# A hand-written order for the second slot of a fused attention and Gelu-MLP kernel

## The chip, the cores and the metric

The kernel runs on one core of one Trainium2 chip. A core has five engines with an instruction queue each: TensorE (PE) for matmuls, VectorE (DVE), ScalarE (ACT), GpSimd (POOL) and SyncE (SP), which here only issues transfers. They run side by side and wait for each other through semaphores. The metric is the device time of one execution in microseconds (us).

## The reference

For each of 8 batches and 8 heads, 512 tokens `x` and 32 state vectors attend to each other; then all 8 × (512 + 32) = 4352 rows, each with the 8 heads side by side (512 numbers), go through a two-layer network with an exact Gelu.

```python
scores = scale * np.matmul(x, state.transpose(0, 1, 3, 2))
a = softmax(scores);   xread = np.matmul(a, state)        # 512 rows a batch
scores2 = scale * np.matmul(state, x.transpose(0, 1, 3, 2))
a2 = softmax(scores2); sread = np.matmul(a2, x)           # 32 rows a batch
x = concatenate([xread, sread], axis=2)  # heads side by side: 4352 x 512
h = x @ w_in                             # w_in 512 x 2048
g = 0.5 * h * (1.0 + erf(h * inv_sqrt2))
return g @ w_out                         # w_out 2048 x 512
```

## The kernel before, in words

All matmuls take bf16 inputs. Instead of forming `xread` and multiplying it by `w_in`, the kernel multiplies the state by `w_in` first: `P = state @ w_in` for each batch (`p_mm`, in four chunks of 512 columns), and then `h = a @ P`. One step of `mm1(b, m)` makes 128 of the 2048 hidden columns for the 512 tokens of a batch: two matmuls (line 478) and one Gelu on ACT (line 485) into `g`. `M(k, ...)` in the code calls `mm1` for the global column block k = 16 × batch + m. The second product of batches 0 and 1 is done in units of four matmuls (`mm2`, line 504): `U(u)` is one unit, for a quarter q of the hidden columns and a quarter j of the rows, where u = 16 × batch + 4 × q + j. The last quarter of a row block is copied out of PSUM by DVE (line 491) and written by SP. From batch 2 on the second product is done by `X`, a scheme with seven block products instead of eight; it needs sums of quarters of `w_out` (`w_sums`, five DVE additions at line 552) and of `g` (`g_sum`, line 580).

The attention of a batch b is prepared one slot ahead. `rearr` (POOL, line 218) puts the tokens into the order that a transposing transfer wants, `xtr_dma` (SP, line 271) transposes them into `xT`, and `rearr_ones` (POOL, line 228) makes the copy `xo` that the state read uses. `scores` makes 16 small matmuls in two halves (line 324) and an exponential on ACT for each half (line 331). `norm` sums, inverts and multiplies on DVE (lines 344, 346 and 347), and `atr_dma` (SP, line 367) transposes the result `a` into `AT`, which `mm1` of that batch reads. `pmat(b, f)` makes one chunk of P: eight matmuls (line 415) and two casts out of PSUM, one on ACT (line 426) and one on DVE (line 427).

The exponential and the Gelu use different function tables of ACT: a table load (1.28 us in the profile) stands ahead of the first of each kind.

Every engine works in the order in which the calls are written; the file fixes this order by hand and there is no planner. A "slot" is the time in which a batch's sixteen M are done, in eight steps of two. The kernel uses eight PSUM tiles of 128 × 512 float32. Four of them (`ps_f`) rotate among the outputs of M, the scores, P chunks and small transposes: the n-th output takes the place of the (n-4)-th and waits until that has been read. The other four (`otile`) hold the second product's sums; some P chunks borrow them as well.

The change concerns the second slot (batch 1's M, numbers 16 to 31), from step 2 on. It is a loop over p = 2 to 7 after line 920. In it `hold` and `load_x(4)` (POOL, the latter a transfer of a batch of tokens) are issued once; the small copy `hold` keeps POOL back until a Gelu has been done, so that the load starts no sooner. After that loop the general one over b = 2 to 7 begins. In its first pass the remaining units of batch 1 are done, two in each of the steps 0 to 3 and one in each step from 4 on, until there are none left. The P chunks of batch 3 come in steps 5 and 7 (`p_run`), the first two of them in borrowed ones.

Of the kernel before, what the change touches and what calls it, by code (L numbers as in the profile page):

```python
# [17 lines left out]
def kernel(  # L18
# [8 lines left out]
    nc = tc.nc  # L27
# [51 lines left out]
    hold = persist.tile([128, 1], BF16, name="hold")  # L79
# [35 lines left out]
    def load_x(b):  # L115
        xb = xin.tile([128, H, SJ * D], BF16, name="xb", tag="xb")
        nc.gpsimd.dma_start(out=xb, in_=xr[b])
        xbs[b] = xb
# [80 lines left out]
    def begin(b):  # L199
        A = Att()  # L200
        atts[b] = A
        A.x4 = x4s[b % 2]
        A.xo = xos[b % 2]
        if b > 0:
            A.xT = att.tile([128, SJ, HC, 128], BF16, name="xT", tag="xT")

    def begin_e(b):
        A = atts[b]
        A.e = att.tile([128, SJ * 2, HC * NS], BF16, name="e", tag="e")
        A.a = att.tile([128, SJ * 2, HC * NS], BF16, name="a", tag="a")  # L210
# [3 lines left out]
    def rearr(b):  # L214
        A = atts[b]
        src = xbs[b].rearrange("p (t c) (j d) -> p t c j d", t=2, d=D)
        for t in range(2):
            nc.gpsimd.tensor_copy(  # L218
                out=A.x4[:, :, :, 64 * t:64 * t + 64].rearrange("p j c d -> p c j d"),
                in_=src[:, t],  # L220
            )

    def rearr_ones(b):
        A = atts[b]
        eng = nc.vector if b < 2 else nc.gpsimd
        src = xbs[b].rearrange("p (t c) (j d) -> p t c j d", t=2, d=D)
        for t in range(2):
            eng.tensor_copy(  # L228
                out=A.xo[:, :, :, 2 + 64 * t:66 + 64 * t].rearrange("p j c d -> p c j d"),
                in_=src[:, t],  # L230
            )
# [37 lines left out]
    def xtr_dma(b):  # L269
        A = atts[b]  # L270
        nc.sync.dma_start_transpose(
            out=A.xT.rearrange("p j c n -> p (j c) n"),
            in_=A.x4.rearrange("p j c n -> p (j c n)"),
        )
# [41 lines left out]
    def scores(b, half):  # L316
        A = atts[b]
        if half == 0:
            begin_e(b)
        pt = ps_f.tile([128, SJ, 2, 2, NS], FP32, name="pt", tag="f")  # L320
        for ci in range(2):
            c = 2 * half + ci
            for j in range(SJ):
                nc.tensor.matmul(  # L324
                    pt[:, j, :, ci, :],
                    lhsT=A.xT[:, j, c, :],
                    rhs=sbd[:, b, c, :],
                    start=True,
                    stop=True,
                )  # L330
        nc.scalar.activation(  # L331
            out=A.e[:, :, 64 * half:64 * half + 64],
            in_=pt.rearrange("p j t c n -> p (j t) (c n)"),
            func=AF.Exp,
            scale=scale,
        )

    def norm(b, half):
        A = atts[b]
        G = SJ * 2  # L340
        hs = slice(64 * half, 64 * half + 64)
        e4 = A.e[:, :, hs].rearrange("p g (c n) -> p g c n", n=NS)
        cs = att.tile([128, G, 2], FP32, name="cs", tag="cs")
        nc.vector.reduce_sum(out=cs, in_=e4, axis=AX.X)  # L344
        ics = att.tile([128, G, 2], FP32, name="ics", tag="ics")
        nc.vector.reciprocal(out=ics, in_=cs)
        nc.vector.tensor_tensor(  # L347
            out=A.a[:, :, hs].rearrange("p g (c n) -> p g c n", n=NS),
            in0=e4,
            in1=ics[:, :, :].to_broadcast((128, G, 2, NS)),  # L350
            op=ALU.mult,
        )
# [11 lines left out]
    def atr_dma(b):  # L364
        A = atts[b]
        A.AT = att.tile([128, SJ, 2, 128], BF16, name="AT", tag="AT")
        nc.sync.dma_start_transpose(
            out=A.AT.rearrange("p j t n -> p (j t) n"), in_=A.a
        )
# [29 lines left out]
    def srt(b):  # L399
        A = atts[b]  # L400
        ps = ps_f.tile([128, HC, NS], BF16, name="srT", tag="f")
        nc.tensor.transpose(
            ps.rearrange("p c n -> p (c n)"), A.srm.rearrange("q t d -> q (t d)"), ident
        )
        nc.vector.tensor_copy(out=XSR[:, :, :, b], in_=ps)  # L405
# [18 lines left out]
    def p_copy(b, f, ps):  # L424
        dst = Ps[b][:, :, f * 512:(f + 1) * 512]
        nc.scalar.copy(out=dst[:, 0, :], in_=ps[0])  # L426
        nc.vector.tensor_copy(out=dst[:, 1, :], in_=ps[1])  # L427

    def pmat(b, f):
        p_copy(b, f, p_mm(b, f, ftile))  # L430
# [40 lines left out]
    gs = {}  # L471
# [82 lines left out]
    def w_sums(i):  # L554
        (b11, b12), (b21, b22) = w_q
        w_add(*(
            ("3", b12, b22, ALU.subtract),
            ("4", b21, b11, ALU.subtract),
            ("6", b11, b12, ALU.add),
            ("1", b11, b22, ALU.add),  # L560
            ("7", b21, b22, ALU.add),
        )[i])
# [245 lines left out]
    def M(*ms):  # L808
        for m in ms:
            mm1(m // MC, m % MC)  # L810

    def U(*us):
        for u in us:
            mm2(u // 16, u % 16 // 4, u % 4)
# [105 lines left out]
    U(16)  # L920


    u = 17
    for p in range(2, 8):
        if p == 4:
            scores(2, 0)
            scores(2, 1)
            norm(2, 0)
            norm(2, 1)
        if p == 7:  # L930
            atr_dma(2)
        if p == 3:
            begin(3)
            rearr(3)
            xtr_dma(3)
            rearr_ones(3)
        M(16 + 2 * p, 17 + 2 * p)
        U(u)
        u += 1
        if p in (5, 7):  # L940
            pmat(2, 2 + p // 7)
        if p >= 3:
            w_sums(p - 3)
        if p == 2:
            nc.gpsimd.tensor_copy(out=hold, in_=gs[1][:, 4, 0:1])
            load_x(4)

    for b in range(2, B):
        nb = b + 1
        for p in range(8):  # L950
            k = 16 * b + 2 * p
            if p == 1 and nb < B:
                scores(nb, 0)
                scores(nb, 1)
            if p in (2, 3) and nb < B:
                norm(nb, p - 2)
            if p == 3 and nb + 1 < B:
                xtr_dma(nb + 1)
            if p == 5 and nb < B:
                atr_dma(nb)  # L960
            if p == 3 and nb < B:
                srt(b)
            if p == 7 and nb == B - 1:
                srt(nb)
            M(k, k + 1)
            if b == 2:
                for _ in range(2 if p < 4 else 1):
                    if u < 32:
                        U(u)
                        u += 1  # L970
            elif p < 5:
                if p == 0:
                    g_sum(b - 1, "5")
                X(b - 1, "45127"[p])
                if p < 3:
                    g_sum(b - 1, "127"[p])
            if nb == B and p < 4:
                for m in range(4 * p, 4 * p + 4):
                    mm1_sr(m)
            if p == 1 and nb < B:  # L980
                sread(b)
                sread_out(b)
            if p == 4 and nb == B - 1:
                sread(nb)
                sread_out(nb)
            if p == 0 and b + 3 < B:
                nc.gpsimd.tensor_copy(out=hold, in_=gs[b][:, 0, 0:1])  # L987
                load_x(b + 3)
            if p == 0 and nb + 1 < B:
                begin(nb + 1)  # L990
                rearr(nb + 1)
            if p == 2 and nb + 1 < B:
                rearr_ones(nb + 1)
            if nb == B:
                if p == 4:
                    r_homes()
                    r_sum("5")
                    r_sum("2")
                if p == 5:
                    g_sum(b, "6")  # L1000
                    R("3")
                    r_sum("1")
                    R("4")
                    r_sum("6")
                    r_sum("7")
                if p == 6:
                    R("5")
                    X(b, "3")
                    R("2")
                    R("1")  # L1010
                if p == 7:
                    R("6")
                    X(b, "6")
                continue
            if p == 5:
                g_sum(b, "6")
                if nb < B:
                    p_run(nb, (0, 1), ((0, 1), (3, 2)))
            if p == 6:
                X(b, "3")  # L1020
            if p == 7:
                if nb < B:
                    p_run(nb, (2, 3), ((1, 2), None))
                X(b, "6")
# [41 lines left out]
```

The softmax here doesn't subtract the row's maximum and nothing guards it: scores larger than these inputs give would overflow.

## Time and profile before

| quantity | value |
|---|---|
| time, median of 13 runs | 209.8 us (209.3 to 211.76) |
| time of the profiled execution | 209.8 us |
| its span, first to last instruction | 208.0 us |
| busy: PE, DVE, ACT, POOL | 96%, 66%, 64%, 30% |
| granted PE clock, mean | 0.997 |
| start of M(20, 21), start of M(32, 33) | 42.02 us, 55.21 us |

A line of the timeline gives the start and the length in us, the engine, the line of the kernel, the operation, what it writes and reads, the shapes, and how many instructions are merged in it; in brackets stands the idle time of the engine before it and what ended that. Matmuls overlap, so the step from one start to the next is what a matmul costs. A line of a tile's view gives the shortest, median and longest duration in ns, then the first and last start.

### The profile page before, as it was taken

To read this page: it belongs to the slowest core of one execution; us is meant where nothing else is said; L and a number is where in the kernel's file an instruction comes from. 1 tells how busy PE (TensorE), PEld (TensorE's weight loads), DVE (VectorE), ACT (ScalarE), POOL (GpSimd) and SP (SyncE) were. 2 spreads that over 40 slices of the span, in tenths; PEclk is the share of its full clock that TensorE was granted. 3 is DMA by queue.
4 is the path that set the end of the run, shared out by engine and by line. 5 is a ranking of instruction groups with operands and counts; after the bars stand their busy time and mean duration, and the time that the engine had idled before them with its cause. 6 is when DMAs were issued, how large, how long until landed. Compare 5 with 4: busy or idle time off the path is not lost.

```text
span 208.0 us, 4691 instructions
## 1 busy us (share of the span) xinstructions
PE 200.6 (96%) x1963; PEld 131.2 (63%) x1971; DVE 137.4 (66%) x218; ACT 133.2 (64%) x240; POOL 62.1 (30%) x69
## 2 busy tenths in 40 slices
PE   7899999998999999999999999999999999999993
PEld 6545444453454567756775677757775788778882
DVE  2944675747919648995699658855887553165872
ACT  3864875679794779565956777587757566744120
POOL 8964300664171015710677005600220001200000
PEclk9999999999999999999999999999999999999998
DMA  6999999689373908736582603360106001030124
GB/s 191 199 181 204 205 195 192 108 221 192 50 99 96 262 0 102 155 123 82 60 167 59 174 0 87 69 202 3 52 3 202 3 0 50 3 151 0 54 102 151
DMA packets 40261, 23.14 MB, mean 111 GB/s; under 512 B 21808, under 2 KB 38320, under 8 KB 40240
## 3 DMA queue, kind: packets, MB, share of 16 engines
q0 software_dynamic: 13936, 8.10, 28.7%
q1 hardware_dynamic: 25616, 14.36, 26.6%
q10 hardware_dynamic: 688, 0.39, 0.6%
q8 instruction: 15, 0.25, 0.5%
q14 instruction: 6, 0.05, 0.1%
HBM read 17.30 MB, written 8.91 MB: 126 GB/s over the span
## 4 chain that ended last, share of the span: by engine, by line
PE 74%; DVE 11%; DMA 5%; POOL 4%; ACT 3%; issue 1%; POOLq 0%; DVEq 0%; ACTq 0%
PE xp L586 28%; PE hp L478 21%; PE op L504 9%; DMA w_out_bf<-in_moe_w_out_dram 5%; DVE gsum L580 5%; PE p_ps L415 4%; PE hps L518 3%; PE rp L764 3%; DVE a L347 2%; POOL w_in_bf L105 2%; PE op L531 2%; DVE cs L344 1%; PE sr L378 1%; POOL sbd L95 1%; PE pt L324 1%
## 5 line engine op out<-in xcount | busy, mean ns | idle before, releaser
L485 ACT ACTIVATE g<-hp 128x512 bf16<-128x512 f32 x124 | 67.6, 602 | 31.6 <-PE hp L478 26.5
L478 PE MATMUL hp<-AT,P 128*128 128x512 bf16 x248 | 64.2, 379 | 0.5 <-DVE XSR L405 0.4
L586 PEld LDWEIGHTS <-gsum 128*128 128x128 bf16 x464 | 45.0, 98 | 11.5 <-issue 2.1
L580 DVE TENSOR_TENSOR gsum<-g 128x2048 bf16<-128x2048 bf16 x30 | 39.3, 1328 | 0.1
L478 PEld LDWEIGHTS <-P 128*128 128x128 bf16 x248 | 22.3, 98 | 21.2 <-issue 4.0
L586 PE MATMUL xp<-ws,gsum 128*128 128x256 bf16 x272 | 32.5, 273 | 0.0
L427 DVE CAST P<-p_ps 128x512 bf16<-128x512 f32 x31 | 20.0, 684 | 15.8 <-PE p_ps L415 15.8
L504 PE MATMUL op<-w_out_bf,g 128*128 128x512 bf16 x90 | 23.0, 379 | 0.4 <-DMA w_out_bf<-in_moe_w_out_dram 0.2
L586 PE MATMUL xp<-ws,g 128*128 128x256 bf16 x192 | 22.9, 273 | 0.0
L586 PE MATMUL xp<-w_out_bf,gsum 128*128 128x256 bf16 x192 | 22.8, 273 | 0.0
L586 PEld LDWEIGHTS <-g 128*128 128x128 bf16 x192 | 18.8, 98 | 4.3
L426 ACT CAST P<-p_ps 128x512 bf16<-128x512 f32 x31 | 16.9, 602 | 6.9 <-PE p_ps L415 6.9
L635 POOL TENSOR_TENSOR u<-s,oh 128x512 f32<-128x512 f32 x5 | 6.3, 1267 | 49.0 <-ACT oh L632 49.0
L504 PEld LDWEIGHTS <-g 128*128 128x128 bf16 x96 | 9.1, 98 | 11.7 <-issue 1.4
L218 POOL COPY x<-xb 128x1024 bf16<-128x1024 bf16 x12 | 12.6, 1083 | 11.3 <-DMA xb<-in_x_dram 11.3
L228 POOL COPY xo<-xb 128x1024 bf16<-128x1024 bf16 x12 | 14.5, 1241 | 1.3 <-PE sr L378 1.3
L347 DVE TENSOR_TENSOR a<-e,ics 128x512 bf16<-128x512 bf16 x14 | 13.9, 994 | 0.5
L344 DVE TENSOR_REDUCE cs<-e 128x16 f32<-128x512 bf16 x14 | 9.5, 677 | 3.8 <-ACT e L331 3.8
L415 PE MATMUL p_ps<-w_in_bf,sbd 64*32 64x512 bf16 x248 | 11.1, 382 | 0.8 <-ACT g L485 0.7
L605 POOL TENSOR_TENSOR v<-q,oh 128x512 f32<-128x512 f32 x5 | 6.4, 1277 | 14.8 <-ACT oh L637 14.8
L629 DVE TENSOR_TENSOR s<-xp,s 128x512 f32<-128x512 f32 x5 | 3.5, 692 | 11.0 <-PE xp L586 11.0
L987 POOL COPY hold<-g 128x1 bf16<-128x1 bf16 x3 | 1.0, 332 | 31.5 <-ACT g L485 31.5
(111 smaller groups left out, 221.2 us busy)
## 6 DMA issues: line engine op xcount, KB each, us to landing
xb<-in_x_dram POOLq DMA_DIRECT2D x7, 512.0 KB, 6.7
out_dram<-oh SPq DMA_DIRECT2D x13, 256.0 KB, 2.5
out_dram<-osb SPq DMA_DIRECT2D x10, 256.0 KB, 3.3
out_dram<-oh SPq DMA_DIRECT2D x5, 512.0 KB, 2.7
w_out_bf<-in_moe_w_out_dram POOLq DMA_DIRECT2D x4, 512.0 KB, 12.2
w_in_bf<-in_moe_w_in_dram POOLq DMA_DIRECT2D x6, 256.0 KB, 11.9
x0f<-in_x_dram SPq DMA_DIRECT2D x3, 256.0 KB, 4.0
w_in_bf<-in_moe_w_in_dram POOLq DMA_DIRECT2D x4, 128.0 KB, 3.9
```

Of the source, the lines that this page charges most:

```text
L218: nc.gpsimd.tensor_copy(out=A.x4[:, :, :, 64 * t:64 * t + 64].rearrange("p j c d -> p c j d"), in_=src[:, t],)
L228: eng.tensor_copy(out=A.xo[:, :, :, 2 + 64 * t:66 + 64 * t].rearrange("p j c d -> p c j d"), in_=src[:, t],)
L344: nc.vector.reduce_sum(out=cs, in_=e4, axis=AX.X)
L347: nc.vector.tensor_tensor(out=A.a[:, :, hs].rearrange("p g (c n) -> p g c n", n=NS), in0=e4, in1=ics[:, :, :].to_broadcast((128, G, 2, NS) ...
L415: nc.tensor.matmul(ps[t][32 * c:32 * c + 32, :], lhsT=sbd[64 * t:64 * t + 64, b, c, 32 * t:32 * t + 32], rhs=w_in_bf[64 * t:64 * t + 64, c ...
L426: nc.scalar.copy(out=dst[:, 0, :], in_=ps[0])
L427: nc.vector.tensor_copy(out=dst[:, 1, :], in_=ps[1])
L478: nc.tensor.matmul(hp, lhsT=Ps[b][:, t, m * 128:(m + 1) * 128], rhs=atts[b].AT[:, :, t, :], start=(t == 0), stop=(t == 1),)
L485: nc.scalar.activation(out=gs[b][:, m, :], in_=hp, func=AF.Gelu)
L504: nc.tensor.matmul(ps, lhsT=gs[b][:, m, j * 128:(j + 1) * 128], rhs=w_out_bf[:, m, :], start=(m == 0), stop=(m == MC - 1),)
L580: nc.vector.tensor_tensor(out=t, in0=g_q(b, h0, k0), in1=g_q(b, h1, k1), op=op)
L586: nc.tensor.matmul(ps[:, j - js[0], :], lhsT=lhs[:, m, 128 * j:128 * j + 128], rhs=rhs[:, m, :], start=(first and j == js[0] and m == 0), ...
```

## The change

The loop over steps 2 to 7 of the second slot is written out, in another order. The chunk `pmat(2, 2)` moves from step 5 to ahead of M(22, 23). The scores of batch 2 come behind M(22, 23) directly, ahead of U(18). U(20) and U(21) stand together behind M(26, 27), and U(23), which was in the next slot, is done ahead of M(32, 33). The sums of `w_out` keep their sequence but are issued sooner: the first before `pmat(2, 2)`, the second and third ahead of `norm(2, 0)`, the fourth behind M(28, 29), and the fifth at the end as before. No instruction is added or removed.

```diff
-    u = 17
-    for p in range(2, 8):
-        if p == 4:
-            scores(2, 0)
-            scores(2, 1)
-            norm(2, 0)
-            norm(2, 1)
-        if p == 7:
-            atr_dma(2)
-        if p == 3:
-            begin(3)
-            rearr(3)
-            xtr_dma(3)
-            rearr_ones(3)
-        M(16 + 2 * p, 17 + 2 * p)
-        U(u)
-        u += 1
-        if p in (5, 7):
-            pmat(2, 2 + p // 7)
-        if p >= 3:
-            w_sums(p - 3)
-        if p == 2:
-            nc.gpsimd.tensor_copy(out=hold, in_=gs[1][:, 4, 0:1])
-            load_x(4)
-
+    M(20, 21)
+    U(17)
+    nc.gpsimd.tensor_copy(out=hold, in_=gs[1][:, 4, 0:1])
+    load_x(4)
+    w_sums(0)
+    pmat(2, 2)
+    begin(3)
+    rearr(3)
+    xtr_dma(3)
+    rearr_ones(3)
+    M(22, 23)
+    w_sums(1)
+    scores(2, 0)
+    scores(2, 1)
+    U(18)
+    w_sums(2)
+    norm(2, 0)
+    norm(2, 1)
+    M(24, 25)
+    U(19)
+    M(26, 27)
+    U(20, 21)
+    M(28, 29)
+    w_sums(3)
+    U(22)
+    atr_dma(2)
+    M(30, 31)
+    U(23)
+    pmat(2, 3)
+    w_sums(4)
+
+    u = 24
     for b in range(2, B):
```

## The prediction

> **What bounds the kernel now.** I read the page first, for the share of each engine and the chain that ended last.
>
> ```profile
> span 208.0 us, 4691 instructions
> PE 200.6 (96%) x1963; PEld 131.2 (63%) x1971; DVE 137.4 (66%) x218; ACT 133.2 (64%) x240; POOL 62.1 (30%) x69
> ...
> PE 74%; DVE 11%; DMA 5%; POOL 4%; ACT 3%; issue 1%; POOLq 0%; DVEq 0%; ACTq 0%
> ```
>
> TensorE (PE) is busy 96% of the span, so the change can win only PE idle time in its own stretch, and it loses whatever new idle time it makes. I therefore read the timeline of the stretch, from M(20, 21) at 42.02 us to M(32, 33), the first work of batch 2, at 55.21. PE alone, from U(17) on:
>
> ```profile
> 42.88 1.03 PE L504 MATMUL op<-w_out_bf,g 128*128 128x512 bf16 x4
> ...
> 45.94 1.03 PE L478 MATMUL hp<-AT,P 128*128 128x512 bf16 x4
> 46.80 1.03 PE L504 MATMUL op<-w_out_bf,g 128*128 128x512 bf16 x4
> 47.89 1.08 PE L478 MATMUL hp<-AT,P 128*128 128x512 bf16 x4
> 48.81 0.81 PE L504 MATMUL op<-w_out_bf,g 128*128 128x512 bf16 x3
> 50.29 0.89 PE L415 MATMUL p_ps<-w_in_bf,sbd 64*32 64x512 bf16 x8 [0.67 <-ACT g L485]
> 51.27 1.08 PE L478 MATMUL hp<-AT,P 128*128 128x512 bf16 x4
> ...
> 55.21 1.04 PE L478 MATMUL hp<-AT,P 128*128 128x512 bf16 x4
> ```
>
> Starts matter here, because matmuls overlap. A pair M and a unit U each move the next start by 0.863 (46.80 - 45.94); the scores take 0.465, a P chunk 0.44. The stretch holds 6 pairs, 6 units, one set of scores and two chunks: 5.18 + 5.18 + 0.47 + 0.88 = 11.71. It lasts 13.19. So 1.48 us are idle, in the starts after 46.80, at 50.29 and within that chunk. Next, who makes PE wait, and the work on the other engines:
>
> ```profile
> 45.95 1.28 ACT L331 ACT_TABLE_LOAD   x1 [0.49 <-PE pt L324]
> ...
> 48.35 1.28 ACT L485 ACT_TABLE_LOAD   x1
> 49.64 2.07 ACT L485 ACTIVATE g<-hp 128x512 bf16<-128x512 f32 x4
> ```
>
> From 45.95 ScalarE (ACT) loads the exponential's table, runs two exponentials, and loads the Gelu's table back; no Gelu runs until 49.64. The four rotating PSUM buffers are then full, and PE waits for their readers.
>
> **The change, part by part.** *A chunk of P ahead of the scores, U(20) to U(23) behind them.* No PE work is added: U(23) only comes before batch 2 instead of in it. I replayed PE with the same steps. U(17) ends at 43.74, the chunk lasts to 44.18, M(22, 23) to 45.05, the scores to 45.51, U(18) to 46.38, M(24, 25) to 47.24, U(19) to 48.10. M(26) takes the first scores' buffer, free at about 47.84, as before; U(20, 21) then run to 50.69, when the Gelu of M(24) has ended (about 50.24). U(22), M(30, 31), U(23) and the last chunk end at 54.58. Every buffer is free by then: the work beside the table loads no longer needs one. ACT keeps its times: the moved cast (0.59) fits between Gelus at 44.31 to 44.90, and the first table load stays at about 45.9. Equal work before (one more unit) stood at 55.21 + 0.86 = 56.07. **Gain: 56.07 - 54.58 = 1.49 us**, if batch 2 may start at 54.58.
>
> *May it?* M(32) needs the transposed attention AT, which SyncE (SP) fetches once both norm(2) are done on VectorE (DVE). Before, the second product of the norms ended at 51.18, the transfer was issued at 51.25 and landed 3.1 us later, at 54.37: 0.84 ahead of its reader. At 54.58 the margin is 0.2. The transfer's time is nearly all spent already, so lateness on DVE reaches PE.
>
> *Sums of w_out sooner.* The second and third sum are put ahead of norm(2, 0) in DVE's order. What waits behind them is the norms, then the AT transfer on SP's queue, then M(32). At their own price they are free:
>
> ```profile
> L552 DVE TENSOR_TENSOR ws<-w_out_bf x5: 1215/1216/1218, 42.9 to 56.0; 128x2048 bf16<-128x2048 bf16 x5
> ```
>
> The chunk's cast ends about 45.03 (44.35 + 0.68), two sums take 2.4, and the first exponential ends at 47.84. But GpSimd (POOL) is not idle there: the batch-3 copies, whose start hangs on the Gelu of M(20) and so doesn't move, run from 44.95 to 48.93. The trace has the same DVE operation, shape and type beside the same copies later (batch 2):
>
> ```profile
> 44.95 2.03 POOL L218 COPY x<-xb 128x1024 bf16<-128x1024 bf16 x2
> 46.91 2.02 POOL L228 COPY xo<-xb 128x1024 bf16<-128x1024 bf16 x2
> ...
> 78.53 2.03 POOL L218 COPY x<-xb 128x1024 bf16<-128x1024 bf16 x2
> 79.12 2.52 DVE L580 TENSOR_TENSOR gsum<-g 128x2048 bf16<-128x2048 bf16 x1
> ...
> 84.07 2.48 POOL L228 COPY xo<-xb 128x1024 bf16<-128x1024 bf16 x2
> 84.10 1.55 DVE L347 TENSOR_TENSOR a<-e,ics 128x512 bf16<-128x512 bf16 x1
> ```
>
> The sum over g took 2.52 instead of 1.22 and ended at 81.64, 1.08 after the second copy's end (80.56): it was shut out for both L218 copies; the sum at 101.25 repeats this (2.61). Beside the L228 pair DVE got in between: the product ended at 85.65, the second copy 0.91 later. In the kernel before, the norms escape, as their products start when POOL is nearly done.
>
> Replay with these rows: the first sum starts at 44.96 against POOL's 44.95, is shut out to 46.98 and ends at 48.06; an xo copy runs to 48.96; the next sum ends at 50.04; the last copy 50.94. The norms, before 47.87 to 51.18, run from 49.96 to about 53.26 (the same 3.3). AT is issued at 53.32, 2.07 late. Its landing takes 3.13 here, but 3.55 and 3.69 in quieter stretches; I take 3.4: 56.72, plus 0.1 for the weight load that waits for it. PE waits 56.82 - 54.58 = **2.24 us**.
>
> Here a rule stands beside the row. The Trainium skill (SBUF — State Buffer, "Who interferes with whom") says that a DVE instruction with two SBUF inputs and a GpSimd instruction that reads SBUF exclude each other, for the length of the holder's instruction. By the rule alone DVE would get in after the first copy, at 46.00, and the same replay ends the norms at 53.05: 0.2 us less. I take the row.
>
> *Sums 4 and 5* follow the norms on DVE; their readers come in batch 2's later steps, beyond 70 us: nothing. The w_out loads have long landed. POOL's tail is about 2 us later (48.93 to 50.94); its xo copies are read first by the batch-3 state read, after 60 us.
>
> *U(31) one step sooner.* In batch 2's step 4 the unit between M(40, 41) and M(42, 43) is gone, so the P chunks of batch 3 follow both pairs directly; their first PSUM tile is the one that U(31) filled. DVE must copy it out first, behind norm(3, 1), the copy after it, and U(30). Before, this copy ended at 69.18 and the chunk started at 69.25. On that clock PE would now arrive at 68.39 and DVE, counted on by 0.67, 0.25, 0.69, 0.73 and 0.6 for each copy-out, finishes at about 68.5. **Cost 0.17 us**, between 0 and 0.4.
>
> **Sum.** -1.49 + 2.24 + 0.17 = +0.9 us. The profiled execution took 209.8 around its span of 208.0, and 209.8 is also the median of the runs: 210.7.
>
> **Rivals.** (1) *No shut-out*: the sums keep 1.22 us, end at about 47.4 before the exponentials, AT lands at 54.4. Then -1.49 + 0.17 = -1.3: 208.5. For it: the sums of w_out before show no delay; against it, none of those ran beside POOL's copies. This rival turns to a loss when the norms are more than 1.4 us late. (2) *Interleaving*: the starts 44.96 and 44.95 are a tie; if DVE goes first and alternates with each copy, the norms end about 52.1, AT lands at 55.2 to 55.8, and the sum is -0.5 to +0.1: about 209.6. Against it: both sums beside L218 copies lost two in a row. (3) *Shut out for all four copies*, to 48.93: sums to 51.15, norms to 54.4, AT at 57.6 to 58.1, hence +1.8 to +2.3: 211.9. Against it is the L228 row. PE would idle 3.1 to 3.7 us. The skill (TensorE: Matmul & The Clock Gate, "HAM oscillation — how this bites in real kernels") sets a limit of about 3.4 us of idling, after which the clock halves; the granted clock is 1.00 all through this stretch, whose longest named wait is 0.67, so no run here shows it. My 2.24 stays under it; (3) might not, and 3.4 us at half speed would cost some 1.7 more.
>
> **Chances.** Forecast 0.50 (own range 210.3 to 211.1, from the landing time and that tile); (1) 0.17; (2) 0.13; (3) 0.12; something unforeseen 0.08, mostly slower. Below 0.3% (0.63 us) this kernel's runs can't tell a change. Slower: 0.42 of the forecast, (3) and most of the rest, 0.60. Same: the forecast's low edge and half of (2), 0.16. Faster: (1) and part of (2), 0.24. The range runs from (1) to (3): 208.5 to 211.9.
>
> **What would show it.** PE without idle from 45 to 54.6 shows the first step right. Sums of w_out at 2 to 3 us beside the L218 copies, norms ending near 53.3, AT landing after 56 and a PE wait of about 2.2 us ahead of M(32) show the loss. Sums at 1.22 us there, or AT landing before 55, would make the prediction wrong.

## The result

The changed kernel takes 212.78 us (median of 11 runs, 211.03 to 213.33) against 210.01 for the kernel before, a ratio of 1.0116 with an interval of 1.0093 to 1.0138: 1.2% slower. The forecast was 210.7, with a range up to 211.9. The sign was right, the size was not. A twelfth execution of the changed kernel, at 213.74, is not in the median, but it is counted where the clock is told below.

The profiled execution took 211.66 around a span of 209.9. From the page of the changed kernel (the span, PE's share, the chain that ended last):

```profile
span 209.9 us, 4691 instructions
PE 200.2 (95%) x1963; PEld 131.2 (63%) x1971; DVE 141.1 (67%) x218; ACT 133.1 (63%) x240; POOL 62.1 (30%) x69
...
PE 74%; DVE 14%; DMA 6%; POOL 3%; issue 2%; DVEq 0%; POOLq 0%
```

PE does the same work in a longer span, and DVE's share of the chain has grown from 11% to 14%. The timeline of PE alone, in the changed kernel:

```profile
45.29 0.63 PE L324 MATMUL pt<-sbd,xT 128*128 128x64 bf16 x16
45.76 1.03 PE L504 MATMUL op<-w_out_bf,g 128*128 128x512 bf16 x4
46.62 1.03 PE L478 MATMUL hp<-AT,P 128*128 128x512 bf16 x4
47.48 0.81 PE L504 MATMUL op<-w_out_bf,g 128*128 128x512 bf16 x3
48.35 1.03 PE L478 MATMUL hp<-AT,P 128*128 128x512 bf16 x4
49.21 1.89 PE L504 MATMUL op<-w_out_bf,g 128*128 128x512 bf16 x8
...
54.48 0.41 PE L415 MATMUL p_ps<-w_in_bf,sbd 64*32 64x512 bf16 x8
57.78 1.04 PE L478 MATMUL hp<-AT,P 128*128 128x512 bf16 x4 [2.89 <-DMA AT<-a]
...
69.14 1.89 PE L478 MATMUL hp<-AT,P 128*128 128x512 bf16 x8
71.11 0.62 PE L415 MATMUL p_ps<-w_in_bf,sbd 64*32 64x512 bf16 x16
```

From 45 to 54.8 the starts follow each other without a gap: the idle time around the table loads is gone. The line at 57.78 has taken its place: PE waits for AT. The start-up is not the same in every execution: M(20) starts at 42.26 here and at 42.02 before, so 0.24 us of any difference of the two traces lies ahead of the change. M(32) could have started at 54.82 (54.48 and 0.34 for the chunk), 54.58 on the clock of before. It starts at 57.78, 2.96 us later.

Who is late shows in the timelines of DVE, POOL and SP of the same execution:

```profile
45.19 5.07 DVE L552 TENSOR_TENSOR ws<-w_out_bf 128x2048 bf16<-128x2048 bf16 x1
45.19 2.03 POOL L218 COPY x<-xb 128x1024 bf16<-128x1024 bf16 x2
47.15 2.03 POOL L228 COPY xo<-xb 128x1024 bf16<-128x1024 bf16 x2
...
53.92 0.69 DVE L347 TENSOR_TENSOR a<-e,ics 128x512 bf16<-128x512 bf16 x1
...
54.68 1.23 SPq L367 DMA_TRANSPOSE AT<-a  x1
```

The second sum takes 5.07 us instead of 1.22. It starts with POOL's first copy and ends at 50.26, 1.08 after the fourth (49.18). The third sum follows, the norms end at 54.62 (their second product starts at 53.92), AT is issued at 54.68 and lands at 57.74.

In the trace this adds up to -1.49 + 2.96 + 0.14 = +1.6 us, the last term being the wait at 71.11 (M(40) to M(43) start at 69.14; four times 0.43 and 0.10 later the chunk could start at 70.97). With the 0.24 of the start-up this is the difference of the spans. The medians lie 2.8 apart, though. The missing part is told by the granted clock of each execution: in 7 of the first 12 (the one at the median among them) its mean is 0.991 or 0.992, and their spans average 211.4; in the other 5, the profiled one among them, it is 0.999 or 1.0, and the spans average 210.1.

### The profile page after: what moved, and what is told of

Its sections match the earlier page's. It is cut to its first block, busy times and chain, and to the rows that moved or that the text cites. A ratio compares the mean times of both kernels' runs of the same rounds, so it can differ in the third digit from the quotient of the medians.

```text
span 209.9 us, 4691 instructions
## 1 busy us (share of the span) xinstructions
PE 200.2 (95%) x1963; PEld 131.2 (63%) x1971; DVE 141.1 (67%) x218; ACT 133.1 (63%) x240; POOL 62.1 (30%) x69
## 4 chain that ended last, share of the span: by engine, by line
PE 74%; DVE 14%; DMA 6%; POOL 3%; issue 2%; DVEq 0%; POOLq 0%
PE xp L586 28%; PE hp L478 21%; PE op L504 8%; DVE gsum L580 5%; DMA w_in_bf<-in_moe_w_in_dram 5%; PE p_ps L415 5%; PE hps L518 3%; PE rp L764 3%; PE op L531 2%; DVE a L347 2%; DVE cs L344 2%; POOL w_in_bf L105 2%; DMA AT<-a 1%; DVE osb L491 1%; PE pt L324 1%
## 5 line engine op out<-in xcount | busy, mean ns | idle before, releaser
L228 POOL COPY xo<-xb 128x1024 bf16<-128x1024 bf16 x12 | 14.6, 1243 | 1.3 <-PE sr L378 1.3
L552 DVE TENSOR_TENSOR ws<-w_out_bf 128x2048 bf16<-128x2048 bf16 x5 | 9.8, 1985 | 0.0
```

Source lines behind the costliest of these rows:

```text
L228: eng.tensor_copy(out=A.xo[:, :, :, 2 + 64 * t:66 + 64 * t].rearrange("p j c d -> p c j d"), in_=src[:, t],)
L552: nc.vector.tensor_tensor(out=w_sum[name], in0=x, in1=y, op=op)
```

## The experiments

Three explanations were to be told apart. **The port** (a short name): POOL's copies shut out DVE's sums, and all else follows. The runs can show that the two exclude each other, not where in the chip they meet. **The order**: the early sums, or the reordered PE work, are harmful by themselves. **The transfer**: AT is late on SP's queue, where the batch-3 transfer now takes 4.0 us to issue. Beside these stands the question of what lowers the clock. The table gives what was measured; "M(20) to M(32)" is free of the start-up, and "low clock" counts the executions with a mean granted clock of 0.992 or less. The ratio of three_more_sums is that of its three executions with full clock; its median includes the fourth.

| kernel | median us | ratio to before (interval) | M(20) to M(32), us | PE wait for AT, us | low clock |
|---|---|---|---|---|---|
| before | 210.0 | 1 | 13.19, one unit less | none | 2 of 76 |
| changed | 212.78 | 1.0116 (1.0093–1.0138) | 15.52 | 2.9 | 8 of 15 |
| sums_behind | 208.73 | 0.9941 (0.992–0.9961) | 12.57 | none | 0 of 11 |
| only_sums_early | 209.62 | 0.9992 (0.9978–1.0006) | 13.19, one unit less | none | 0 of 20 |
| xo_copies_later | 209.65 | 0.9983 (0.9965–1.0001) | 13.58 | 0.94 | 1 of 20 |
| copies_first | 208.21 | 0.9923 (0.9894–0.9951) | 12.57 | none | 0 of 6 |
| second_sum_first | 208.93 | 0.9956 (0.993–0.9982) | 13.16 | none | 0 of 9 |
| only_chunk_early | 209.35 | 0.9978 (0.9961–0.9995) | 12.84, one unit less | under 0.2 | 0 of 11 |
| three_more_sums | 212.3 | 1.0103 (1.0076–1.0129) | 15.68 | 3.01 | 1 of 4 |
| four_more_sums | 215.26 | 1.0266 (1.0241–1.0291) | 16.89 | 4.25 | 4 of 4 |
| unit_kept_back | 208.28 | 0.9932 (0.9908–0.9956) | 12.57 | none | 0 of 5 |

**The early sums undone (sums_behind).** Against the changed kernel:

```diff
-    w_sums(1)
     scores(2, 0)
     scores(2, 1)
     U(18)
-    w_sums(2)
     norm(2, 0)
     norm(2, 1)
+    w_sums(1)
+    w_sums(2)
```

> The changed kernel with one thing undone: the second and third sum of w_out stand behind both norm(2) on DVE again, as before. If the port is the cause (the second sum, 5.07 us long, is shut out by POOL's four copies, and so the norms, the AT transfer and M(32) are late), the norms end near 51.2 us, AT lands near 54.4, PE waits less than 0.2 us ahead of M(32), and the reordering shows its gain: 1.3 us less span than the kernel before (-1.49, +0.17 for the tile of U(31)), a time near 208.5 to 208.7. The mean granted clock then stays at 0.997 or more in every run. If the reordered PE work or the SP queue (its xT transfer now takes 4.0 us to issue) were the cause, AT would still land after 56 and the time stay above 211.

It is faster than the kernel before by 0.6%, and every execution has a clock of 0.998 or more. The timeline:

```profile
51.79 3.49 DVE L552 TENSOR_TENSOR ws<-w_out_bf 128x2048 bf16<-128x2048 bf16 x3
51.93 1.23 SPq L367 DMA_TRANSPOSE AT<-a  x1
...
54.96 0.41 PE L415 MATMUL p_ps<-w_in_bf,sbd 64*32 64x512 bf16 x8
55.30 1.04 PE L478 MATMUL hp<-AT,P 128*128 128x512 bf16 x4
```

Three sums in a row now take 3.49 us, beside no copy. M(20) starts at 42.73 here, 0.71 later than before, so AT, landing at 55.04, is at 54.33 on the clock of before, and M(32) starts at 55.30, or 54.59: the 54.58 of the replay. The transfer of batch 3 still takes 4.08 us to issue, and AT is on time: the transfer is not the cause, and neither is the reordered PE work.

**The sums as early as in the change, the copies elsewhere (copies_first).**

```diff
+    begin(3)
+    rearr(3)
+    rearr_ones(3)
     M(20, 21)
     U(17)
...
     pmat(2, 2)
-    begin(3)
-    rearr(3)
     xtr_dma(3)
-    rearr_ones(3)
```

> The changed kernel, sums as early as there, but POOL's four copies of batch 3 stand ahead of the small copy that waits for a Gelu and ahead of load_x(4), so that they run from about 40 to 44 us, before the second sum. Port as the cause: the second and third sum last 1.22 us each, although nothing in DVE's order is changed; the first one may be shut out instead, to about 45. The norms end at 51.2 to 51.5, AT lands at 54.4 to 54.8, PE waits at most 0.3 us, and the span is 0.9 to 1.3 us under the kernel before. If the early sums are harmful by their own length, AT stays late.

```profile
38.84 2.02 POOL L218 COPY x<-xb 128x1024 bf16<-128x1024 bf16 x2
40.80 2.03 POOL L228 COPY xo<-xb 128x1024 bf16<-128x1024 bf16 x2
...
44.63 2.35 DVE L552 TENSOR_TENSOR ws<-w_out_bf 128x2048 bf16<-128x2048 bf16 x2
47.52 0.69 DVE L344 TENSOR_REDUCE cs<-e 128x16 f32<-128x512 bf16 x1 [0.54 <-ACT e L331]
```

DVE's order is that of the changed kernel, to the instruction. The copies run from 38.84 to 42.83, sooner than expected. The two sums take 2.35 together, DVE is idle for 0.54 until the exponential, and the wait for AT is gone. Only the place of the copies differs (they are now also ahead of `hold` and `load_x(4)`). This shows the meeting of copies and sums to be the cause. The kernel is the fastest of all, if only just (unit_kept_back, built on it, is 0.1 us apart): 0.8% under the kernel before, 1.9% under the changed one. The first sum, which meets the end of the copies, pays 0.14 for it here, and 0.5 to 0.6 in the three later traces with the same order up to there.

**Two of four copies taken away from the sum (xo_copies_later).**

```diff
     xtr_dma(3)
-    rearr_ones(3)
     M(22, 23)
...
     M(28, 29)
+    nc.gpsimd.tensor_copy(out=hold, in_=gs[1][:, 12, 0:1])
+    rearr_ones(3)
     w_sums(3)
```

> The changed kernel with POOL's two xo copies of batch 3 kept back until the Gelu of M(28) is done; only the two x copies are left to stand against the second sum. Port as the cause: the second sum ends 1.08 us after the second x copy and lasts about 3.1 us instead of 5.07, the norms end near 52.6, AT lands near 56, PE waits 1.1 to 1.6 us ahead of M(32) instead of 2.9, and the span equals that of the kernel before within 0.4 us. A wait this short should not bring the low mean clock (0.991) that most runs of the changed kernel show. If something else makes AT late, the PE wait stays near 2.9.

```profile
45.26 3.10 DVE L552 TENSOR_TENSOR ws<-w_out_bf 128x2048 bf16<-128x2048 bf16 x1
...
55.91 1.04 PE L478 MATMUL hp<-AT,P 128*128 128x512 bf16 x4 [0.94 <-DMA AT<-a]
```

With two copies queued the sum is shut out for two: 3.10 us, as expected. AT lands at 55.86 and PE loses 1.02 us (55.91 - 54.89), a little less than the 1.1 to 1.6 expected. The gain of the new order and this wait nearly cancel.

**The early sums alone, in the order of before (only_sums_early).** `w_sums(1)` ahead of `scores(2, 0)` and `w_sums(2)` ahead of `norm(2, 0)`, all else as before.

> The kernel before with only one part of the change: the second and third sum of w_out ahead of the scores and of norm(2, 0). There is no P cast between the first and the second sum here, so the second starts at 44.0, ahead of POOL's first copy, and keeps 1.22 us; the third then meets all four copies. Port as the cause: the third sum lasts 4 to 5 us, to about 50.3, the norms end near 53.6, AT lands near 56.8, PE waits 1.5 us ahead of M(32), and the span is 1.5 us over the kernel before. If DVE gets in after each copy, the third sum lasts 2 to 2.3 us and the span is 0 to 0.6 over. If the sums are harmless, no difference.

```profile
44.72 3.16 POOL L218 COPY x<-xb 128x1024 bf16<-128x1024 bf16 x2
44.92 2.06 DVE L552 TENSOR_TENSOR ws<-w_out_bf 128x2048 bf16<-128x2048 bf16 x1
47.82 2.49 POOL L228 COPY xo<-xb 128x1024 bf16<-128x1024 bf16 x2
```

The port theory in the form that I had given it failed here: the third sum was not shut out for four copies. It took 2.06 us, got in behind the first copy, and ended at 46.98, ahead of the exponential. PE saw nothing of it, and the time is that of before. The copies show the difference: the two x copies take 3.16 instead of 2.03, as the first waited for the second sum, which had started at 43.79, and the second for the third sum.

**The second sum started ahead of the first copy (second_sum_first).** In the changed kernel `w_sums(1)` stands directly behind `w_sums(0)`, ahead of `pmat(2, 2)`.

> The changed kernel with the second sum one place sooner on DVE, directly behind the first one and ahead of the P cast; the third stays ahead of the norms. The second sum then starts at 44.0, ahead of POOL's first copy, and that copy has to wait for it, as in only_sums_early. If POOL and DVE take turns once a copy has had to wait, the third sum lasts about 2 us or less, the norms are on time, PE has no wait ahead of M(32), and the span is 0.9 to 1.3 us under the kernel before (the cast is 0.5 us later, which may hold up the second half of the scores). If what counts is that the sum asks while copies stand queued, the third sum is shut out to about 49.2, lasts 4 to 5 us, and PE waits 1.5 to 2 us; the span is 0.2 to 0.6 over the kernel before.

```profile
44.46 3.16 POOL L218 COPY x<-xb 128x1024 bf16<-128x1024 bf16 x2
45.26 1.45 DVE L552 TENSOR_TENSOR ws<-w_out_bf 128x2048 bf16<-128x2048 bf16 x1
...
45.39 0.39 PE L324 MATMUL pt<-sbd,xT 128*128 128x64 bf16 x8 [0.43 <-DVE P L427]
```

This is the first of the two outcomes that were expected: again the copy had to wait for a sum, and again the next sum got in after one copy, although three more were queued: 1.45 us. The cast behind the sum is late and holds up the second half of the scores by 0.4 us and more, which is the 0.59 between this kernel and the best one (13.16 against 12.57). One place in DVE's queue thus decides between 5.07 and 1.45 us for the sum behind.

**The chunk alone (only_chunk_early).** The kernel before, with `w_sums(0)` and `pmat(2, 2)` ahead of M(22, 23).

> The kernel before with the P chunk ahead of M(22, 23) (and the first sum ahead of it, as in the change); the units and the other sums stay. By the same replay as in the prediction, M(26, 27) still wait for the exponentials and M(28, 29) for the first Gelus behind the table load, so about 1.0 of the 1.48 us of PE idle stays: M(32) could start 0.5 us sooner, and AT, 0.45 late, holds it up by at most 0.2. Span 0.3 to 0.55 us under the kernel before. If the chunk is what fills the gap, 1.3 or more; if the scores' tiles matter more than the order, no gain.

M(20) to M(32) shrinks by 0.35 us: within what was expected. The chunk by itself is a small part of the 1.49; most of it needs the units behind the scores.

**More idle time of PE, without the copies (three_more_sums, four_more_sums).** In copies_first, three or four further additions, which write a sum of `w_out` anew, stand ahead of the norms:

```diff
     w_sums(2)
+    for _ in range(3):
+        nc.vector.tensor_tensor(
+            out=w_sum["6"], in0=w_q[0][0], in1=w_q[0][1], op=ALU.add
+        )
     norm(2, 0)
```

> copies_first (the fastest so far, with no PE wait here) with three more additions of the same kind, shape and length ahead of norm(2, 0), which write a sum of w_out anew; there are no POOL copies beside them. It brings back the late norms without the port: norms about 3.2 us later, a PE wait of about 2.9 us ahead of M(32), a span 2.6 to 3.0 us over copies_first (209.0 to 209.4) where the clock holds. If the idle PE is what lets the clock drop, about half of the executions or more show a mean clock near 0.992 and another 1.2 us. If the low clock belongs to the port conflict or to the changed kernel's order, none do.

> As three_more_sums, with four additions: a PE wait of about 4.2 us. If the idle PE is what lets the clock drop, nearly all executions have a mean clock near 0.992 or below, and the span is 3.9 us + about 1.2 us over copies_first. Otherwise the clock stays at 0.997 to 1.0 and the span is 3.9 us over.

The late norms bring the PE wait back without a port conflict: M(32) starts 3.11 and 4.32 us later than in copies_first. With 4.25 us of waiting all four executions have the low clock. From the timeline of PE in four_more_sums:

```profile
58.55 1.89 PE L478 MATMUL hp<-AT,P 128*128 128x512 bf16 x4 [4.25 <-DMA AT<-a]
60.23 2.77 PE L504 MATMUL op<-w_out_bf,g 128*128 128x512 bf16 x8
```

The four matmuls at 58.55 take 1.89 us instead of 1.03: half clock. It lasts from 58.58 to 61.99. Of three_more_sums, where I expected half of the executions or more, one of four had it, for two stretches of 3.4 us (57.40 to 64.22). Its other three have spans of 209.8 to 210.5, somewhat above the 209.0 to 209.4 expected. So the low clock belongs to the idle time and not to the port, which has no part in four_more_sums; four executions are too few for a share.

**The changed kernel again, for a trace with the low clock (changed_again, changed_third, changed_fourth).** The kernel is unaltered.

> The changed kernel once more, unaltered, for its trace. Of its first twelve executions eight had a mean granted clock of 0.991 or 0.992 and spans of 211.0 to 211.9, four had 0.999 or 1.0 and 209.3 to 210.6; the profiled one was of the second kind. If the PE wait for AT lets the clock drop, an execution of the first kind shows one stretch of 3.4 us at half clock within a few us behind the wait at about 57 us, and the 1.2 us that it is longer lie there. If the low clock comes from elsewhere (start, end), the stretch behind the wait looks as before. An execution of the second kind decides nothing.

> The changed kernel unaltered, for a trace of an execution with the low mean clock, which changed_again didn't give. If the PE wait lets the clock drop here as it did in three_more_sums and four_more_sums, an execution with a mean clock near 0.992 shows one stretch of 3.4 us at half clock that begins within the wait or up to 3.4 us behind its end, and a span of 211.0 to 211.9. With a mean clock of 0.999 or 1.0 it decides nothing.

> As changed_third: the same kernel and the same question, once more.

The first text miscounts: it was seven of the first twelve, and five of the other kind. All three traces repeat the long second sum and a PE wait of 2.9. The first two kept the clock (spans 210.1 and 210.3); the third has a mean of 0.992 and a span of 211.6. Its PE timeline, then its stretches from the view that adds up busy time by windows (behind the window stand its length and PE's busy time; the seventh item is the granted clock, ahead of the DMA share and rate):

```profile
57.84 1.04 PE L478 MATMUL hp<-AT,P 128*128 128x512 bf16 x4 [2.88 <-DMA AT<-a]
58.72 3.56 PE L504 MATMUL op<-w_out_bf,g 128*128 128x512 bf16 x8
```

```profile
55.36:58.77 3.41, 0.93 (x5) 0.46 (x6) 2.17 (x3) 0.47 (x2) 0.00 (x0) 1.00 0.41 77
58.77:62.18 3.41, 3.41 (x11) 1.21 (x10) 0.00 (x0) 2.14 (x3) 2.58 (x4) 0.50 0.27 20
```

Two units take 3.56 us instead of 1.89. Half clock holds from 58.77 to 62.18, one stretch of 3.41 us that begins 0.9 behind the end of the wait. It costs 1.7 us: from the start of M(32) to the end of the span are 153.8 us here and 152.1 in the three traces of this kernel with full clock. That is more than the 1.3 between the mean spans of the two kinds, which also contain start-ups of different length.

**A unit put back (unit_kept_back).** In copies_first, the line that spreads the units over batch 2's slot becomes `for _ in range(2 if p < 3 else 1)`.

> copies_first with the units of batch 2's slot spread as two, two, two, one, one over its first five steps, instead of two in each of four: a unit again stands between M(40, 41) and M(42, 43), as in the kernel before. If the P chunks of batch 3 wait there for DVE to copy out U(31), as the prediction's third term says, the 0.14 to 0.16 us of PE idle ahead of them go and the span falls by about 0.15 against copies_first; the time can hardly show it. If nothing waits there, no difference in the trace.

```profile
66.58 1.03 PE L478 MATMUL hp<-AT,P 128*128 128x512 bf16 x4
67.67 0.63 PE L415 MATMUL p_ps<-w_in_bf,sbd 64*32 64x512 bf16 x16
```

The chunk could start 0.96 behind 66.58, at 67.54, and starts at 67.67: the wait of 0.13 stays, and so does the span, 206.4. DVE works without a gap from norm(3, 1) to the copy-out of U(31), which ends at 67.62, wherever PE has the unit: the copy-out of U(29), which stood behind norm(3, 1) in the kernel before and now stands ahead of it, is what pushes it. That is read from the traces; no run puts this copy back.

## Why the prediction was right or wrong

*"Gain: 56.07 - 54.58 = 1.49 us."* Right: 54.58 in the changed kernel, 54.59 in sums_behind, both on the clock of before. There is no idle time beside the table loads.

*"Lateness on DVE reaches PE"*, by way of the sums, the norms and AT. Right, and shown by undoing either side of the conflict.

*"Beside the L228 pair DVE got in between."* **This step failed.** I took from one pair of rows that the sum would enter behind two of the four copies, at 46.98. It entered behind the last, and ended at 50.02 on the clock of before instead of 48.06. The norms ended at 54.38 instead of 53.26. Rival (3), shut out for all four copies, is what happened. I had put it at 0.12, since one row spoke against it. But that row is of another instruction: the product of the norms (line 347, 128x512, 0.69 us alone), not a sum of 128x2048. The rows with a sum beside two queued copies, at 79.12 and 101.25, both have it shut out for both.

*"Its landing takes 3.13 here ... I take 3.4."* It took 3.06; the nearest row would have been better than the middle of several.

*"PE waits 2.24 us."* 2.96: 1.1 more by the failed step, 0.4 less by the landing and the weight load behind it, two errors that in part cancel. Rival (3) gave 3.1 to 3.7.

*"Cost 0.17 us"* for U(31). 0.14, but the reason was wrong in part: the order of DVE's queue causes the wait, not the place of the unit on PE.

*"My 2.24 stays under it; (3) might not."* **This step failed too**: it put the clock's term at nothing for any wait under 3.4 us. The Trainium skill (TensorE: Matmul & The Clock Gate, "HAM oscillation — how this bites in real kernels") names 3.4 us of idling. Here 2.9 us were enough in 8 of 15 executions, so 3.4 is no safe limit. The price was the 1.7 that I estimated. The same page ("What's actually happening") states that the activity is judged in windows of about 3.4 us which run freely, and the traces agree: by the traces' records of the clock, the time between two changes of it is always a whole number of 3.413 us (in changed_fourth full clock for 16 of them, up to 58.77, half clock for one, full clock for 44). Laid on this grid, the trace of the changed kernel and the end of that of the kernel before read:

```profile
53.25:56.67 3.42, 1.64 (x15) 0.50 (x12) 3.35 (x6) 1.67 (x3) 0.00 (x0) 1.00 0.25 48
56.67:60.08 3.41, 2.29 (x11) 1.09 (x12) 0.81 (x1) 1.57 (x3) 0.54 (x2) 1.00 0.16 28
...
203.50:206.92 3.42, 1.24 (x18) 0.93 (x16) 1.01 (x3) 0.00 (x0) 0.00 (x0) 1.00 0.65 210
206.92:208.03 1.11, 0.00 (x0) 0.00 (x0) 0.00 (x0) 0.00 (x0) 0.00 (x0) 0.50 0.00 0
```

In the first two windows the wait is split, 1.77 us of idle PE in one and 1.12 in the other, and the clock holds. In changed_fourth 2.48 us fell into one window (55.36 to 58.77, above), and the clock halved at its end. Over all 14 traces, no window at full clock with up to 1.77 us of idle PE has a halving behind it, and each one with 2.0 or more has. So what counts here is the idle time within one window, with a limit between 1.8 and 2.0 of its 3.41 us, and for a wait of 2.9 its place in the windows decides. (Moved over the trace of the changed kernel, such windows would halve the clock in 67 to 81% of their positions, an estimate; 8 of 15 were counted.) The 2.24 of the forecast is above this limit, so it was not safe either. The kernel before could have told: its clock halves at 206.92, behind a window with 2.18 us of idle PE.

**The sum.** For rival (3) without the clock it was +1.8 to +2.3; the trace has +1.6. Six of the eleven executions behind the median have the low clock; six elevenths of 1.7 are 0.9 more, 2.5 in all, against 2.4 from the ratio of 1.16%. The range ended at 211.9, the middle of rival (3), and held nothing for the clock, which the text had priced. The wait alone would have stayed within it (210.0 + 1.6 = 211.6; the five executions with full clock average 211.86); the clock is what carried the time out of it.

## What to carry to other kernels

An instruction that is moved to fill a queue's idle time has to be checked for what the neighbouring engine does in that window: the same addition took 1.22, 1.45, 2.06, 3.10 and 5.07 us here, by what POOL had queued and who came first. Ahead of a transfer that lands just in time, price the lateness at the transfer's reader. And a new PE wait of 2 us or more can cost more than itself, as the clock may halve behind it (1.7 us more here); a mean clock that differs between executions of one kernel is the sign. A row that stands in for an instruction should be of the same instruction.

## What the runs showed of the hardware

**A queue of copies can shut a sum out for its whole length.** The Trainium skill (SBUF — State Buffer, "Who interferes with whom") has the holder keep a shared pair of ports for the length of its instruction, and the other engine wait. Here a sum that arrived with the first of four queued copies was shut out for all four (5.07 us, in each of four traces of the changed kernel), and for both when there were two (3.10). When the copy that ran had itself waited for DVE, the next sum got in behind that one copy (2.06 and 1.45), and from then on the two engines took turns. For sums this holds without exception in all 14 traces: 33 that met a copy which had not waited were shut out for every copy behind it too, and 16 that met one which had (at 129.59 in the kernel before, behind a copy of 1.50 us instead of 1.04) got in. The product of the norms (line 347) got in behind the first copy in all 30 cases in which it met two, though none of these copies had waited, as at 84.10 in the kernel before. So the kind of instruction seems to count as well; but those cases also differ in what POOL did just before, and no run separates the two. What decides stays open.

**The clock halves in stretches of 3.41 us** (6.83 once). In the three executions that were traced they begin within a PE wait of 2.9 us or more or up to 1 us behind its end, behind a window of 3.41 us in which PE was idle for 2.0 us or more. The low mean clock came in 8 of 15 executions at a wait of 2.9, 1 of 4 at 3.0, 4 of 4 at 4.25, which leaves over 2.1 us in one window wherever it falls. With a wait of 0.94 it was 1 of 20, with none 0 of 62 in the variants and 2 of 76 in the kernel before; of these three there is no trace, and their cause is open.
